# Retention and a gated feed-forward layer in one kernel: k and q of two pairs loaded ahead of v, first gates in halves of 256 tokens, idle products of 128 columns

## The chip, the cores and the metric

The kernel runs on one core of a Trainium2 chip. A core has five engines that run beside each other and meet at semaphores: TensorE (PE in the profile; its weight loads are PEld), VectorE (DVE), ScalarE (ACT), GpSimd (POOL) and SyncE (SP), which here only issues DMAs. SBUF is the working memory, PSUM holds the accumulators of TensorE in banks of 512 float32 numbers per partition. The metric is the device time of one execution in microseconds (us).

## The reference

Retention: 8 batches, 8 heads, 576 positions, 64 numbers per head. Then a feed-forward layer on the 4608 tokens of 512 numbers.

```python
scores = scale * np.matmul(q, k.transpose(0, 1, 3, 2))
Dmat = np.where(rel >= 0, gamma[:, None, None] ** rel[None, :, :], 0.0)
attn_out = np.matmul(scores * Dmat[None, :, :, :], v)
x = attn_out.transpose(0, 2, 1, 3).reshape(B * S, H * D)
gate = 1.0 / (1.0 + np.exp(-(x @ w_gate)))
val = x @ w_val
out = (gate * val) @ w_out
```

The decay `gamma ** (i - j)` is a product of a factor for the query's position and one for the key's, so the kernel multiplies q and k by tables once, and only needs a triangular mask inside a chunk of 128 positions and a running state (k transposed times v) between chunks.

## The kernel before, in words

The work has two parts. The **opening** takes the first 768 tokens as three *pairs* of two chunks each (`PAIRS`: batch 0 positions 0 to 255, batch 0 positions 256 to 511, batch 1 positions 0 to 255), and while they run the weights come in. The **main loop** (L789) takes the other tokens in blocks of 256 to 512, and between pieces of a block's feed-forward work it runs the retention of later chunks (`STEPS`, numbered from 0) by a list (`order`).

The order in each engine's queue is the order of the Python code: nothing is scheduled automatically. Every engine takes its instructions in that order, and a wait holds back all that stands behind it on the engine.

All loads go through SP's queue (L105, L114, L126, L132), each of 256 KB. `load_pair` (L109) is a generator that yields after each load: k, q, k, q, v, v of a pair (two halves of the heads). Before, the queue is: the six of pair 0, the six of pair 1, then the weights for blocks 0 and 1 (`load_w(0, 2)`), for 2 and 3, 4 to 7, 8 to 11, then `wo` mixed with pair 2, then the loads of the steps.

For a pair the opening does these things, with g the half of the heads and a the chunk:
- `cast_pair` (L232): k times its table on GpSimd, q times its table on DVE, v to bf16 on GpSimd.
- `turn` (L599, through `pair_t`, L306): four TensorE products against the identity turn k or q round, ACT copies the result to SBUF (kT, qT).
- `pair_qk` (L323): 16 products of k and q into two banks, then two DVE products with the mask `trip` (L335) give `ptp`.
- `pair_intra` (L361): `ptp` times v into `pvp`; `pair_inter` (L375) adds the state of the chunk before times q.
- `pair_st` (L338): 16 products add this chunk to the state `st`; `tile_sv` (L351) copies the state to SBUF with two copies, and the next `pair_st` may not write until they are done.
- `pair_out` (L383): `pvp` to `xT`, the input of the feed-forward layer, by one engine or in halves by DVE and ACT.

`fill(n)` (L154) issues n products of a zero tile, 128x128 by 128x512, into a fresh bank of the pool `ffn`; nobody reads them. They occupy TensorE where it would otherwise stand.

`h_both` (L602) does the feed-forward's first half for the first 512 tokens: for each of the 12 blocks of 128 of the 1536 hidden numbers, four products of 512 columns with `w_gate` (`hg`) and a sigmoid on ACT, and four with `w_val` (`hv`) and a DVE product of both. Blocks 0 and 1 (L683 to L687) have `pair_st(1, 1)` between their first and second group; blocks 2 and 3, 4 to 7 and 8 to 11 follow (L694, L699, L718). `cast_w` (L216) turns the loaded weights to bf16 just ahead; the second half of `wv` for blocks 0 and 1 is cast by DVE (L681). Beside blocks 8 to 11 pair 2 is turned (L721 to L729), and `op_first` (L742) does the output product with `wo`.

After its casts of `wo`, GpSimd goes on with the steps: `cast_k`, `cast_q` and `cast_v` (L244 to L274) fill `qk_nat` and `vbd`, SP issues a DMA transpose of `qk_nat` into `T` (`cross`, L285), and TensorE's `phase_qk` (L391) multiplies on `T`. PSUM has eight banks: one for `tr`, two for `qk`, one for `pv`, one for `st` and three for `ffn`.

The functions that the diff touches follow.

Of the kernel before, what the change touches and what calls it, by code (L numbers as in the profile page):

```python
# [9 lines left out]
FP32 = mybir.dt.float32  # L10
BF16 = mybir.dt.bfloat16
# [5 lines left out]
def kernel(  # L17
# [91 lines left out]
    def load_pair(A):  # L109

        b, a2 = PAIRS[A]
        for nm, src, g in (("k", k, 0), ("q", q, 0), ("k", k, 1), ("q", q, 1), ("v", v, 0), ("v", v, 1)):
            t = ld_pool.tile([P, M, 2, D], FP32, tag="ld", name=f"{nm}32p_{A}_{g}")
            nc.sync.dma_start(  # L114
                out=t.rearrange("p h r d -> p h (r d)"),
                in_=src[b, g * M:(g + 1) * M, a2 * 2 * P:(a2 + 1) * 2 * P, :].rearrange("h (p r) d -> p h (r d)", r=2))
            parts[nm, "pair", A, g] = t
            yield
# [13 lines left out]
        nc.sync.dma_start(out=t, in_=moe_w_out[f * P:(f + 1) * P, :])  # L132
        parts["o", f] = t

    for A in range(2):
        for _ in load_pair(A):
            pass
    load_w(0, 2)
    load_w(2, 2)
    load_w(4, 4)  # L140
# [7 lines left out]
    LEAD_CAST = 3  # L148


    blank = consts.tile([P, 512], BF16)
    nc.vector.memset(blank, 0.0)

    def fill(n):  # L154

        ps = ffn_psum.tile([P, 512], FP32, tag="ffn", name=f"idle_{fill.at}")
        fill.at += 1
        for i in range(n):
            nc.tensor.matmul(ps, lhsT=blank[:, 0:P], rhs=blank, start=True, stop=True)  # L159

    fill.at = 0
    fill(10)
    def tables(shape, pattern, step, put):

# [67 lines left out]
    def cast_pair(nm, A, g, eng):  # L232

        if (nm, A) not in natural:
            natural[nm, A] = osb_pool.tile([P, 2, H, D], BF16, tag="osb", name=f"{nm}p_{A}")
        o = natural[nm, A][:, :, g * M:(g + 1) * M, :].rearrange("p r h d -> p h r d")
        i = parts.pop((nm, "pair", A, g))
        if nm == "v":
            eng(out=o, in_=i)
        else:  # L240
            tab = (ktab2 if nm == "k" else qtab2)[:, PAIRS[A][1], g * M:(g + 1) * M, :].unsqueeze(3).to_broadcast([P, M, 2, D])
            eng.tensor_tensor(out=o, in0=i, in1=tab, op=ALU.mult)
# [58 lines left out]
    def half(x):  # L301
        return slice(x * 64, x * 64 + 64)
# [20 lines left out]
    def pair_qk(A, g, banks):  # L323
        ps = [psum.tile([P, 2, 2, P], FP32, tag=tag, name=f"qkp_{A}_{g}_{hh}") for hh, (psum, tag) in enumerate(banks)]
        for i in range(2):
            m = 2 * g + i
            for r in range(2):
                for a in range(2):
                    for hh in range(2):
                        nc.tensor.matmul(ps[hh][half(a), i, r, :], lhsT=turned["kp", A][half(hh), m, r, half(a)],  # L330
                                         rhs=turned["qp", A][half(hh), m, a * P:(a + 1) * P], start=True, stop=True)
        if g == 0:
            probs["p", A] = att_pool.tile([P, 2, M, 2, P], BF16, tag="ptp", name=f"ptp_{A}", bufs=1)
        for hh in range(2):
            nc.vector.tensor_tensor(out=probs["p", A][:, hh, 2 * g:2 * g + 2], in0=ps[hh],  # L335
                                    in1=trip.unsqueeze(1).to_broadcast([P, 2, 2, P]), op=ALU.mult)
# [21 lines left out]

    pair_ps = {}

    def pair_intra(A, g, a):  # L361
        s = 2 * A + a
        if g == 0:
            pair_ps[s] = (tr_psum if a else pv_psum).tile([P, M, P], FP32, tag="tr" if a else "pv", name=f"pvp_{s}")
        ps = pair_ps[s]
        for i in range(2):
            m = 2 * g + i
            for r in range(2):
                for hh in range(2):
                    nc.tensor.matmul(ps[half(hh), m, :], lhsT=natural["v", A][half(a), r, 2 * m + hh, :],  # L370
                                     rhs=probs["p", A][half(a), hh, m, r, :],
                                     start=(m == 0 and r == 0), stop=(m == M - 1 and r == 1),
                                     skip_group_check=True)

    def pair_inter(A, a):  # L375
        b, a2 = PAIRS[A]
        c = 2 * a2 + a
        for m in range(M):
            nc.tensor.matmul(pair_ps[2 * A + a][:, m, :], lhsT=state[b, c - 1, 1][:, m, :],
                             rhs=turned["qp", A][:, m, a * P:(a + 1) * P],  # L380
                             start=False, stop=(m == M - 1), skip_group_check=True)

    def pair_out(A, a, eng):  # L383
        t0 = (2 * A + a) * P
        if eng is not None:
            eng(out=xT[:, :, t0:t0 + P], in_=pair_ps[2 * A + a])
            return
        for g, half_eng in enumerate((on_dve, on_act)):
            half_eng(out=xT[:, 2 * g:2 * g + 2, t0:t0 + P], in_=pair_ps[2 * A + a][:, 2 * g:2 * g + 2])

    def phase_qk(s):  # L391
        n = width[STEPS[s][1]]
# [206 lines left out]
    def turn(nm, A, g, pool=ffn_psum, tag="ffn"):  # L599
        pair_t(nm, A, g, pool, tag, on_act)  # L600
# [20 lines left out]
        for _ in range(n):  # L621
            next(units)

    cast_pair("k", 0, 0, nc.gpsimd)
    cast_pair("q", 0, 0, nc.vector)
    cast_pair("k", 0, 1, nc.gpsimd)
    cast_pair("q", 0, 1, nc.vector)
    cast_pair("v", 0, 0, on_pool)
    cast_pair("v", 0, 1, on_pool)
    cast_pair("k", 1, 0, nc.gpsimd)  # L630
    cast_pair("k", 1, 1, nc.gpsimd)
    cast_pair("v", 1, 0, on_pool)
    cast_pair("v", 1, 1, on_pool)
    QK = [(qk_psum, "qk"), (qk_psum, "qk")]
    turn("k", 0, 0)
    turn("q", 0, 0)
    fill(4)
    turn("k", 0, 1)
    pair_qk(0, 0, QK)
    turn("q", 0, 1)  # L640
    fill(3)
    pair_qk(0, 1, QK)
    pair_intra(0, 0, 0)
    pair_intra(0, 0, 1)
    pair_st(0, 0)
    tile_sv(0, 0, (on_act, on_act))
    cast_pair("q", 1, 0, nc.vector)
    cast_pair("q", 1, 1, nc.vector)
    fill(2)
    turn("k", 1, 0)  # L650
    pair_intra(0, 1, 0)
    pair_intra(0, 1, 1)
    fill(2)
    pair_inter(0, 1)
    turn("q", 1, 0)
    pair_out(0, 0, on_act)
    pair_st(0, 1)
    fill(1)
    turn("k", 1, 1)
    pair_out(0, 1, on_dve)  # L660
    turn("q", 1, 1)
    pair_qk(1, 0, QK)
    tile_sv(0, 1, (on_act, on_act))
    fill(3)
    pair_qk(1, 1, QK)
    fill(1)
    pair_intra(1, 0, 0)
    pair_inter(1, 0)
    pair_intra(1, 0, 1)
    pair_st(1, 0)  # L670
    tile_sv(1, 0, (on_act, on_act))
    fill(2)
    pair_intra(1, 1, 0)
    pair_out(1, 0, on_act)
    pair_intra(1, 1, 1)
    pair_inter(1, 1)
    pair_out(1, 1, None)
    for i in range(2):
        cast_w("g", 0, 2, i, on_pool)
    cast_w("v", 0, 2, 0, on_pool)  # L680
    cast_w("v", 0, 2, 1, on_dve)  # L681

    units = h_both((0, 1))  # L683
    step(units, 1)
    pair_st(1, 1)
    tile_sv(1, 1, (on_act, on_act))
    step(units, 3)  # L687
    for i in range(2):
        cast_w("g", 2, 2, i, on_pool)
    cast_w("v", 2, 2, 0, on_pool)  # L690
# [143 lines left out]
```

## Time and profile before

| what | value |
|---|---|
| median of 4 runs | 337.01 us (336.96 to 337.23) |
| the profiled execution: its own time, its span | 337.23 us, 335.5 us |
| PE busy in the span | 326.2 us (97%) |
| DVE, ACT, POOL busy | 164.1, 168.3, 185.9 us |
| granted TensorE clock | 1.00 |
| PE busy from 5.0 to 19.7 us | 12.34 of 14.70 us |
| PE busy from 23.7 to 41.9 us | 18.15 of 18.20 us |
| PE busy from 41.9 to 57.7 us | 15.19 of 15.80 us |

All later times are counted from the start of the span. The page gives the busy share of each engine and the chain of work that ended last; the timeline gives instructions in order of time, with the idle time of the engine before them and what ended it in brackets. A row such as `x4` merges four instructions: its second number is from the start of the first to the end of the last. "SPq" rows are issues of DMAs; the landing of a DMA is told by its time to landing, or by who waited for it.

### The profile page before, as it was taken

What the parts mean: (1) busy time and instruction counts of PE and PEld (TensorE: products, weight loads), DVE (VectorE), ACT (ScalarE), POOL (GpSimd) and SP (SyncE); (2) the same over time, 40 slices, a digit from 0 to 9 for tenths busy, and PEclk for the clock granted to TensorE, in tenths of its full rate; (3) what the DMA queues carried; (4) which work ended last, traced back from release to release, by engine and by line L of the source; (5) the groups of instructions that cost most, each with busy time, mean ns of one, the idle gap of its engine ahead of it and who ended that gap; (6) DMA issues with size and microseconds to landing.
All of it is one profiled execution on the core that took longest, in us unless ns stands there. A gap on an engine that the chain in (4) does not pass through costs nothing.

```text
span 335.5 us, 7361 instructions
## 1 busy us (share of the span) xinstructions
PE 326.2 (97%) x2749; PEld 184.7 (55%) x2784; DVE 164.1 (49%) x328; ACT 168.3 (50%) x345; POOL 185.9 (55%) x327
## 2 busy tenths in 40 slices
PE   8899999999999999999999999999999999999996
PEld 3544445969666566556566555454555455454443
DVE  6644755726376356436346635542674156503320
ACT  6545635637565456355456655445646455233321
POOL 4665769789878978773448976482577500000000
PEclk9999999999999999999999999999999999999999
DMA  8999996999999999999986999499773850020002
GB/s 215 314 374 364 323 259 126 153 214 209 170 221 187 171 209 210 213 225 225 218 151 123 193 247 190 100 229 249 136 137 81 252 205 2 0 95 33 0 31 96
DMA packets 164100, 60.00 MB, mean 179 GB/s; under 512 B 144480, under 2 KB 156000, under 8 KB 164064
## 3 DMA queue, kind: packets, MB, share of 16 engines
q1 hardware_dynamic: 163920, 59.39, 85.1%
q8 instruction: 22, 0.36, 0.5%
q14 instruction: 14, 0.11, 0.1%
q10 hardware_dynamic: 144, 0.13, 0.1%
HBM read 37.75 MB, written 9.44 MB: 141 GB/s over the span
## 4 chain that ended last, share of the span: by engine, by line
PE 93%; DMA 2%; DVE 1%; issue 1%; SPq 1%; ACT 0%; POOL 0%
PE h L495 48%; PE op L561 24%; PE hg L610 3%; PE op L745 3%; PE hv L610 3%; PE pv L420 2%; PE qk L399 2%; PE pv L418 2%; DMA k32p<-in_k_dram 2%; PE st L432 2%; SPq L114 1%; PE op L551 1%; PE pvp L370 1%; PE st L345 0%; PE idle L159 0%
## 5 line engine op out<-in xcount | busy, mean ns | idle before, releaser
L495 PE MATMUL h<-xT,wg_sb 128*128 128x384 bf16 (+2 forms) x476 | 102.4, 336 | 0.4 <-DVE gv L523 0.2
L495 PE MATMUL h<-xT,wv_sb 128*128 128x384 bf16 (+2 forms) x473 | 102.2, 336 | 0.4
L252 POOL TENSOR_TENSOR qk_nat<-k,ktab 64x256 bf16<-64x256 f32 x120 | 73.4, 612 | 42.9 <-PE st L432 27.2
L523 DVE TENSOR_TENSOR gv<-g,h 128x384 bf16<-128x384 bf16 (+1 forms) x96 | 59.6, 621 | 71.8 <-PE h L495 56.0
L561 PE MATMUL op<-wo_sb,gv 128*128 128x512 bf16 x356 | 84.5, 379 | 0.8
L519 ACT ACTIVATE g<-h 128x384 bf16<-128x384 f32 (+1 forms) x96 | 52.3, 545 | 64.7 <-PE h L495 58.1
L438 DVE CAST sbd<-st 64x256 bf16<-64x256 f32 x104 | 43.7, 420 | 45.1 <-PE st L432 42.9
L495 PEld LDWEIGHTS <-wg_sb 128*128 128x128 bf16 x480 | 43.7, 98 | 31.4 <-issue 0.4
L495 PEld LDWEIGHTS <-wv_sb 128*128 128x128 bf16 x480 | 44.1, 98 | 29.0 <-issue 0.4
L273 POOL CAST vbd<-v 64x256 bf16<-64x256 f32 x120 | 47.6, 397 | 14.8 <-PE pv L420 10.3
L561 PEld LDWEIGHTS <-gv 128*128 128x128 bf16 x372 | 34.3, 98 | 36.3
L538 ACT COPY ob<-op 128x512 f32<-128x512 f32 x33 | 19.4, 587 | 47.4 <-PE op L561 39.2
L283 ACT CAST vs<-v 64x256 bf16<-64x256 f32 x104 | 42.1, 405 | 1.6
L262 POOL TENSOR_TENSOR qk_nat<-q,qtab 128x512 bf16<-128x512 f32 (+1 forms) x34 | 35.4, 1041 | 2.6
L422 ACT CAST xT<-pv 128x512 bf16<-128x512 f32 (+1 forms) x34 | 18.2, 535 | 18.1 <-PE pv L420 18.0
L401 DVE TENSOR_TENSOR pt<-qk,tri 128x512 bf16<-128x512 f32 (+1 forms) x34 | 21.2, 625 | 6.1 <-PE qk L399 5.8
L420 PE MATMUL pv<-pt,vbd 128*128 128x64 bf16 x240 | 18.0, 193 | 0.0
L432 PEld LDWEIGHTS <-qk_nat 128*128 128x128 bf16 x208 | 13.2, 98 | 8.7
L420 PEld LDWEIGHTS <-vbd 128*128 128x128 bf16 x240 | 15.2, 98 | 3.6
L418 PE MATMUL pv<-T,sbd 128*128 128x64 bf16 x216 | 17.2, 193 | 0.0
L511 DVE TENSOR_TENSOR gv<-g,h 128x256 bf16<-128x256 bf16 x24 | 10.0, 420 | 13.7 <-ACT g L509 13.4
L418 PEld LDWEIGHTS <-sbd 128*128 128x128 bf16 x216 | 15.1, 98 | 2.5
(76 smaller groups left out, 233.5 us busy)
## 6 DMA issues: line engine op xcount, KB each, us to landing
out_dram<-ob SPq DMA_DIRECT2D x34, 256.0 KB, 2.8
v<-in_v_dram SPq DMA_DIRECT2D x26, 256.0 KB, 4.0
k<-in_k_dram SPq DMA_DIRECT2D x26, 256.0 KB, 4.5
q<-in_q_dram SPq DMA_DIRECT2D x26, 256.0 KB, 5.0
wg<-in_moe_w_gate_dram SPq DMA_DIRECT2D x12, 256.0 KB, 5.7
wv<-in_moe_w_val_dram SPq DMA_DIRECT2D x12, 256.0 KB, 5.4
wo<-in_moe_w_out_dram SPq DMA_DIRECT2D x12, 256.0 KB, 5.4
k32p<-in_k_dram SPq DMA_DIRECT2D x6, 256.0 KB, 5.8
```

What stands on the lines that cost most here:

```text
L252: nc.gpsimd.tensor_tensor(out=kn[half(hh), j, :, half(hh)], in0=k32[half(j), hh::2, :], in1=ktab[half(j), c, hh::2].unsqueeze(2).to_broadc ...
L262: nc.gpsimd.tensor_tensor(out=qs[0:n], in0=q32[0:n], in1=qtab[0:n, c, :].unsqueeze(2).to_broadcast([n, H, D]), op=ALU.mult)
L273: nc.gpsimd.tensor_copy(out=vb[half(hh), j, :, half(hh)], in_=v32[half(j), hh::2, :])
L283: nc.scalar.copy(out=natural["vs", s][half(hh), j], in_=loaded[s][0][half(j), hh::2, :])
L401: nc.vector.tensor_tensor(out=pt[:, :, 0:n].rearrange("p m (j t) -> p m j t", t=64), in0=qkp[:, :, 0:n].rearrange("p m (j t) -> p m j t", ...
L418: nc.tensor.matmul(pvp[:, m, half(j)], lhsT=before[:, m, :], rhs=qT[:, m, half(j)], start=True, stop=False)
L420: nc.tensor.matmul(pvp[:, m, half(j)], lhsT=vb[:, j, m, :], rhs=pt[:, m, half(j)], start=before is None, stop=True)
L438: nc.vector.tensor_copy(out=sb[half(hh), :, half(hh)], in_=st_tiles[b][half(hh)])
L495: nc.tensor.matmul(out, lhsT=w_sb[:, kc, fc * P:(fc + 1) * P], rhs=xT[:, kc, t0 + a:t0 + e], start=(kc == 0), stop=(kc == NKC - 1))
L519: nc.scalar.activation(out=g[:, 0:n], in_=h1[:, 0:n], func=AF.Sigmoid)
L523: nc.vector.tensor_tensor(out=gvs[some[0]][:, a:e], in0=g[:, 0:n], in1=h2[:, 0:n], op=ALU.mult)
L561: nc.tensor.matmul(opp, lhsT=gvs[fc][:, nb * P:(nb + 1) * P], rhs=wo_sb[:, fc, :], start=(fc == 0), stop=(fc == NFC - 1))
```

## The change

It does five things.

1. `load_pair` of pairs 0 and 1 is drawn in turn: k, q, k, q of pair 0, the same of pair 1, then v, v of pair 0 and v, v of pair 1. GpSimd's casts are in that order too: all four k, then all four v, then the weights of blocks 0 and 1, now all four on GpSimd.
2. The opening is written in another order: the turns and `pair_qk` of pair 1 ahead of the products that need v; `pair_qk` alternates between the banks `qk` and `ffn`; the turns use the banks `tr` and `pv`; `pvp` of the last chunk lies in two banks; `ptp` has two buffers.
3. Blocks 0 and 1 of the feed-forward layer are done in halves of 256 tokens (`h_half`, `gate`), the first of them among `pair_inter(1, 1)` and `pair_st(1, 1)`. Sixteen products of 512 columns become 32 of 256.
4. `fill(n)` issues 4 n products of 128 columns, all into one tile. The sum of all n goes from 28 to 21.
5. `pair_out` takes one engine or several, each with its share of the head pairs.

PE's program has 144 rows more (5714 instead of 5570, weight loads counted). The rest of the kernel, from `cast_w("g", 2, 2, ...)` on, is the same text.

```diff
-    for A in range(2):
-        for _ in load_pair(A):
-            pass
+    both = [load_pair(A) for A in range(2)]
+    for n_pair in (4, 2):
+        for one in both:
+            for _ in range(n_pair):
+                next(one)
...
-    blank = consts.tile([P, 512], BF16)
+    blank = consts.tile([P, P], BF16)
...
+    idle = ffn_psum.tile([P, 512], FP32, tag="ffn", name="idle")
+
     def fill(n):
-        ps = ffn_psum.tile([P, 512], FP32, tag="ffn", name=f"idle_{fill.at}")
-        fill.at += 1
-        for i in range(n):
-            nc.tensor.matmul(ps, lhsT=blank[:, 0:P], rhs=blank, start=True, stop=True)
+        for i in range(4 * n):
+            nc.tensor.matmul(idle[:, 0:P], lhsT=blank, rhs=blank, start=True, stop=True)
...
+    def pair_tile(A, a, banks):
+        s = 2 * A + a
+        ps = [psum.tile([P, M // len(banks), P], FP32, tag=tag, name=f"pvp_{s}_{i}") for i, (psum, tag) in enumerate(banks)]
+        pair_ps[s] = [(ps[m * len(banks) // M], m % (M // len(banks)), M // len(banks)) for m in range(M)]
...
+    for A in range(2):
+        for g in range(2):
+            cast_pair("k", A, g, nc.gpsimd)
+    for A in range(2):
+        for g in range(2):
+            cast_pair("v", A, g, on_pool)
+    for i in range(2):
+        cast_w("g", 0, 2, i, on_pool)
+    for i in range(2):
+        cast_w("v", 0, 2, i, on_pool)
+    QK = [(qk_psum, "qk"), (qk_psum, "qk")]
+    FF = [(ffn_psum, "ffn"), (ffn_psum, "ffn")]
+    TR, PV = (tr_psum, "tr"), (pv_psum, "pv")
     cast_pair("q", 0, 0, nc.vector)
+    turn("k", 0, 0, *TR)
+    turn("q", 0, 0, *PV)
+    fill(3)
     cast_pair("q", 0, 1, nc.vector)
     pair_qk(0, 0, QK)
+    turn("k", 0, 1, *TR)
+    fill(2)
+    turn("q", 0, 1, *PV)
     fill(3)
+    cast_pair("q", 1, 0, nc.vector)
+    pair_qk(0, 1, FF)
+    turn("k", 1, 0, *TR)
+    turn("q", 1, 0, *PV)
+    fill(2)
+    cast_pair("q", 1, 1, nc.vector)
+    turn("k", 1, 1, *TR)
+    pair_qk(1, 0, QK)
+    fill(1)
+    turn("q", 1, 1)
     pair_intra(0, 0, 0)
     pair_intra(0, 0, 1)
     pair_st(0, 0)
     tile_sv(0, 0, (on_act, on_act))
     pair_intra(0, 1, 0)
+    pair_qk(1, 1, FF)
     pair_intra(0, 1, 1)
+    pair_st(0, 1)
     pair_inter(0, 1)
     pair_out(0, 0, on_act)
     pair_out(0, 1, on_dve)
     tile_sv(0, 1, (on_act, on_act))
     pair_intra(1, 0, 0)
+    pair_tile(1, 1, QK)
     pair_intra(1, 0, 1)
+    pair_intra(1, 1, 0)
     pair_st(1, 0)
     tile_sv(1, 0, (on_act, on_act))
+    pair_inter(1, 0)
+    pair_out(1, 0, on_dve)
     pair_intra(1, 1, 1)
...
+    g0 = h_bank(ffn_psum, "ffn", "hg_0", 1)[:, 0]
+    h_half("g", 0, 0, g0)
+    gate(0, 0, g0)
     pair_inter(1, 1)
+    pair_out(1, 1, on_dve, on_act)
+    g1 = h_bank(ffn_psum, "ffn", "hg_1", 1)[:, 0]
+    h_half("g", 1, 0, g1)
+    gate(1, 0, g1)
     pair_st(1, 1)
     tile_sv(1, 1, (on_act, on_act))
+    v0 = h_bank(ffn_psum, "ffn", "hv_0", 2)
+    h_half("v", 0, 0, v0[:, 0])
+    h_half("g", 0, 1, (g2 := h_bank(qk_psum, "qk", "hg_2", 2))[:, 0])
+    h_half("g", 1, 1, g2[:, 1])
+    h_half("v", 1, 0, v0[:, 1])
+    gate(0, 1, g2[:, 0])
+    gate(1, 1, g2[:, 1])
+    for fc in range(2):
+        h_half("v", fc, 1, h_bank(ffn_psum, "ffn", f"hv_{1 + fc}", 1)[:, 0])
```

`h_half(what, fc, x, ps)` is four products of 256 columns for half x of the tokens, and for `"v"` the DVE product into `gv`; `gate` is the sigmoid on ACT.

## The prediction

> **What bounds the kernel now.** I read the page first. Its first part and its chain say that this is a TensorE kernel.
>
> ```profile
> PE 326.2 (97%) x2749; PEld 184.7 (55%) x2784; DVE 164.1 (49%) x328; ACT 168.3 (50%) x345; POOL 185.9 (55%) x327
> PE 93%; DMA 2%; DVE 1%; issue 1%; SPq 1%; ACT 0%; POOL 0%
> ```
>
> PE is busy for 97% of the span, so nearly all of it is work that this change leaves alone. Time can only be won where PE stands or runs idle products: the opening. I therefore took the chain of work that ended last, in order of time, for the first 24 us.
>
> ```profile
> 4.05 6.07 DMA k32p<-in_k_dram
> 10.19 1.05 POOL kp L242
> 11.29 0.40 PE kTp L311 x4
> ...
> 19.13 0.44 DVE xT L389
> 19.70 1.02 PE hg L610 x4
> ...
> 23.79 1.73 PE hg L610 x8
> ```
>
> The seventh load (k of pair 1) lands at 4.05 + 6.07 = 10.12, and GpSimd starts on it at 10.19, so 0.07 after a landing its user runs. From there to the first gate product at 19.70 PE strings together pair 1. The gates of blocks 2 and 3 (`hg`, second group) start at 23.63 in the timeline, and from there PE has no wait worth the name until the end: the waits of PE after 57 us add up to 0.2 us. So what counts is, first, how much earlier that second group starts, and second, whether anything later holds PE at a fixed time. For the second question I read the timeline of GpSimd and of SP's issues from 46 to 58 us.
>
> ```profile
> 46.31 0.61 POOL L224 CAST wo_sb<-wo 128x512 bf16<-128x512 f32 x1 [0.79 <-DMA wo<-in_moe_w_out_dram]
> ...
> 47.67 1.84 POOL L781 MEMSET vbd<- 128x1024 bf16 x2
> 49.59 2.66 POOL L252 TENSOR_TENSOR qk_nat<-k,ktab 64x256 bf16<-64x256 f32 x4
> 52.32 1.04 POOL L262 TENSOR_TENSOR qk_nat<-q,qtab 128x512 bf16<-128x512 f32 x1
> ```
> ```profile
> 53.39 1.54 SPq L289 DMA_TRANSPOSE T<-qk_nat  x1
> ```
> ```profile
> T<-qk_nat SPq DMA_TRANSPOSE x1, 3.8
> ```
> ```profile
> 57.72 0.40 PE L399 MATMUL qk<-T 128*128 128x64 bf16 x8
> ```
>
> This is a chain without PE in it. GpSimd waits for the last `wo` load, casts it, clears two tiles, casts k and q of the first later step, and SP issues the transpose when the q cast ends (52.32 + 1.04 = 53.36). The transpose takes 3.8 us to land (DMA view of that window): 57.2. PE's first `qk` on it starts at 57.72. **PE reaches that product with only 57.72 - 57.2 - 0.07 = 0.45 us to spare.**
>
> **The change part by part.**
>
> *Order of loads.* All twelve are 256 KB in the same pattern, so I take the landings by place in the queue. Starts of the casts that waited for DMA in the trace: 3.75, 4.57, 6.00, 7.42, 8.37, 9.25, 10.19, about 11.05, 12.01, 12.84, 13.74, 14.59, then the first weights at 15.46. k and q of pair 1 thus come at 8.37 to 11.05 instead of 10.19 to 12.84, v of pair 0 at 12.01 and 12.84 instead of 8.37 and 9.25. Weights keep their places.
>
> *The opening, recomputed.* The turns and masks of both pairs now run while v is on its way: PE meets kp(1,1) at 10.19 + 1.04, qp(1,1) on DVE at about 12.1, and the last turn copy (0.74) ends near 13.4. From v a chain follows: v cast 12.84 + 0.61 = 13.45; 16 state products 0.44, 13.95; two copies of the state 0.75, 14.7; next state 0.44, 15.2; on ACT the xT copy 0.59 stands ahead, so the copies run 15.3 to 16.05; third state to 16.55; its copies to 17.3; inter 0.40; xT halves 0.42 and 0.37, 18.2. Beside it the masks of (1,1) end at 15.6 (two of 0.64 each after PE's products at 14.1), which frees the two DVE copies of xT by 17.5.
>
> *Gates of 256 tokens.* The first needs xT of pair 0 (16.3) and the wg casts, which end at 15.46 + 1.37 = 16.83 as before: it runs 16.9 to 17.35 between the state products, where PE would stand. The second wv cast moves from DVE (19.48 in the trace) to GpSimd behind the first (16.96 + 0.61) and its landing: about 18.3. So the first value product starts at 18.35 instead of 21.90. Thirty-two products of 256 columns replace sixteen of 512: four of 256 take 0.44 from start to start (L495 rows near 56 us), so 8 x 0.44 = 3.5 against 3.45, nothing. Six groups are left at 18.35: 18.35 + 6 x 0.44 = 21.0. **The second group of gates starts at 21.0 instead of 23.63: a lead of 2.6 us.** ACT gets four sigmoids of 0.39 for two of 0.60 and DVE four products of 0.42 for two of 0.69: 0.36 and 0.3 us more, beside PE, whose next use of those tiles is 20 us off; without that cover they would cost as much.
>
> *Idle products.* Twenty-eight of 512 columns become 84 of 128, so a quarter of the number times 3. The first ten units take the same 4.45 us (kTp of 128 columns start 0.107 apart in the slow stretch, a fourth of 0.43); a smaller `blank` (0.27 us now, at least the 0.06 of a small memset) brings them up to 0.2 forward, which the load of k(0,1) at 6.00 swallows. I take 0; both ends are 0 to -0.2.
>
> *Banks, `bufs=2`, one idle tile.* They take away waits on accumulators within the opening and issue nothing. Cost 0, already in the times above.
>
> *What takes the lead back.* At 37.44 PE turns k of pair 2; its cast starts at 34.70 and ends at 35.74, behind GpSimd's memset and the landing, with no PE in it. PE comes there at 37.44 - 2.6 = 34.85 and waits to 35.8: the lead is now 1.64. At `qk` of step 0 it would be at 57.72 - 1.64 = 56.08, but the transpose lands at 57.2, so PE goes on at 57.27. **Of 2.6 us, 0.95 go at the turn, 1.19 at the transpose, and 0.45 are left.** The third transpose (issued 63.09, 4.1 us) lands at 67.2; PE wants it at 67.74 - 0.45 = 67.29, just in time. The others have over a microsecond of room. After that PE hands the 0.45 through to the end.
>
> Sum: the profiled execution took 337.23 (span 335.5, 1.7 around it); 337.23 - 0.45 = 336.78. It stands 0.22 above the median of 337.01, so against the median I say **336.6**. That is 0.13%, under the 0.2% (0.67 us) that a measurement of this kernel can about tell from no change.
>
> *The unknown: when the transpose lands.* Its age in the window 50 to 75 us is 3.3 to 4.7 us, so 0.5 less or 0.9 more than the 3.8 I use. And the program's own instruction blocks (queue 8: 22 packets, 0.36 MB) go through the same DMA engines. The one at 20.5 to 21.9 was followed by a wg cast that waited 0.91 and started at 23.59, 2.18 after the pair before it at 21.41, where later pairs (24.95, 26.31, 27.66, 29.01) stand 1.35 apart; so a block can cost a load some 0.8; the one near 12.5 moved nothing. The change adds 144 rows to PE's 5570, all before the gates, so each block is asked for earlier: by row number I place them near 10, 15, 24.5 and 44 us in place of 12.5, 20.8, 39.7 and 49.6. Three blocks before the last `wo` load become four, but one leaves the neighbourhood of that load. Bounds: the load 0.85 later or 0.85 earlier; I keep 0, between them. [...]
>
> *The clock.* The idle products start 0.43 us apart up to 6.2 us and 0.217 after it ((1.03 - 0.38) / 3 in the row of four at 6.25), so PE does run at half speed at first. After the last fill (about 12.2 us) the new order holds under 3 us of PE work in the 4.7 us up to the gates. [...] In the trace PE stood up to 0.5 us at a time between 6 and 20 us without its products getting slower; the longest stand that I foresee is 0.7, so I count no loss. From the two spacings, 16 gate products of 512 at 0.43 instead of 0.217 would cost 3.4 us, the far end.
>
> **Rivals.**
>
> - *The gate moves forward* (20%). The block near 40 us no longer delays the last loads, the transpose lands 0.4 to 0.85 earlier, PE gains 0.85 to 1.3: 335.7 to 336.2. For: the loads before 46 are one unbroken stream. Against: the new block near 44 us.
> - *The lead passes* (8%): PE keeps 1.64 or more: 335.4 or below. It needs the transpose 1.2 earlier, and nothing in GpSimd's chain gets shorter.
> - *A block falls on the last `wo` load or on the transpose itself* (15%), at 44 to 46 us or 53 to 57. Price 0.85 to 1.75 (one block, or one and the longest transpose age); from 0.45 on it is slower than before. One block: +0.4, 337.4; with the long transpose +1.3, 338.3.
> - *The opening doesn't get shorter* (7%), by the clock or by a wait that I missed: if the lead at the gates is under 0.45, the gain is what is left, 0; with the clock halved through the gates 3.4 - 2.6 = 0.8 slower, 337.8.
>
> **How the numbers follow.** The forecast (gain 0 to 0.67) has 50%. Faster by over 0.2%: the forward gate, the passed lead and a few in a hundred from the forecast's edge, 0.31. Slower by over 0.2%: half of the third rival and part of the last, 0.13. Within: 0.56. The range takes the forward gate in up to a 1.1 us gain and the one-block loss, 335.9 to 337.5.
>
> **What would show it.** The second group of gates starts at 21 to 22; `kTp` of pair 2 waits for GpSimd near 35; PE stands about 1 us before the first `qk` of L405, released by the DMA of T; after it every PE row is 0.4 to 0.5 earlier than before. I am wrong if PE doesn't stand there, if the last `wo` cast leaves 46.3 by more than half a microsecond, or if the gates start after 23.

## The result and the profile after

The changed kernel takes **338.34 us** (median of 52 runs, 336.52 to 339.58) against 337.20 of the kernel before beside it (72 runs, 336.62 to 338.61): the ratio is 1.0031, with a 95% interval of 1.0024 to 1.0037. It is slower, by about 1.1 us, where 336.6 had been forecast.

The median hides two groups. Each execution records its mean granted TensorE clock. Of the 53 on record, the profiled one among them, 19 have 1.00, and their median is 337.44 us; in 33 it is 0.985 to 0.990, and their median is 338.69; one lies between. None of the 128 executions of the kernel before that ran beside the experiments has a clock under 0.998. So there are two losses: about 0.2 us with the clock full (337.44 against 337.20), and 1.2 us more (338.69 - 337.44) wherever the clock falls, which is in six executions of ten.

The execution profiled for the page was one at full clock: 337.44 us, span 335.7. Its busy line and its chain by engine are:

```profile
PE 325.3 (97%) x2824; PEld 190.1 (57%) x2856; DVE 165.2 (49%) x330; ACT 168.5 (50%) x346; POOL 186.3 (55%) x328
PE 80%; DMA 11%; POOL 3%; SPq 2%; issue 1%; DVE 1%; ACT 0%
```

TensorE works 0.9 us less than before (325.3 against 326.2), and the span is 0.2 us longer. The chain has moved from TensorE to the transfers: DMA held 2% of it, now 11%. The timeline of TensorE shows where (start, duration, engine, line, operation, tiles, shape, count; in brackets the idle time before it and what ended it).

```profile
13.66 0.37 PE L346 MATMUL st<-vp,kp 64*64 64x64 bf16 x12 [0.55 <-POOL vp L240]
21.39 1.89 PE L616 MATMUL hg<-xT,wg_sb 128*128 128x512 bf16 x7
36.61 0.40 PE L312 MATMUL kTp<-ident,kp 128*128 128x128 bf16 x4 [1.20 <-POOL kp L243]
40.40 0.38 PE L312 MATMUL qTp<-ident,qp 128*128 128x128 bf16 x4 [0.36 <-ACT qT L322]
57.92 0.41 PE L405 MATMUL qk<-T 128*128 128x64 bf16 x8 [0.34 <-DMA T<-qk_nat]
```

The second group of gates starts at 21.39 instead of 23.63: the opening did get 2.24 us shorter. Then TensorE stands 1.20 us for the cast of k of pair 2, 0.36 for a copy at the turn of its q, and 0.34 for the first transpose, and meets that transpose's product at 57.92, where before it was at 57.72. By the starts of the rows, before and after, the lead goes 1.41 us at the first place, 0.53 at the second and 0.50 at the third. **A lead of 2.24 us has become a lag of 0.20**, and the profiled execution ends 0.21 later (337.44 against 337.23). The last row, in the chain of work that ended last (start, duration, engine, what):

```profile
53.54 4.33 DMA T<-qk_nat
57.92 0.41 PE qk L405 x8
```

SP issues the transpose 0.15 later than before (53.54, 53.39), and it is in flight for 4.33 us instead of 3.8.

That is the loss at full clock. The other one, the clock, cannot be seen in this profile at all; the first experiment was to catch it.

### The profile page after: what moved, and what is told of

It reads as the page before. It is cut to its first block, busy times and chain, and to the rows that moved or that the text cites. A ratio compares the mean times of both kernels' runs of the same rounds, so it can differ in the third digit from the quotient of the medians.

```text
span 335.7 us, 7513 instructions
## 1 busy us (share of the span) xinstructions
PE 325.3 (97%) x2824; PEld 190.1 (57%) x2856; DVE 165.2 (49%) x330; ACT 168.5 (50%) x346; POOL 186.3 (55%) x328
## 3 DMA queue, kind: packets, MB, share of 16 engines
HBM read 37.75 MB, written 9.44 MB: 141 GB/s over the span
## 4 chain that ended last, share of the span: by engine, by line
PE 80%; DMA 11%; POOL 3%; SPq 2%; issue 1%; DVE 1%; ACT 0%
PE h L501 48%; PE op L567 24%; DMA wv<-in_moe_w_val_dram 5%; DMA wo<-in_moe_w_out_dram 3%; SPq L114 2%; PE pv L426 2%; PE qk L405 2%; PE pv L424 2%; PE st L438 2%; DMA v32p<-in_v_dram 2%; DMA T<-qk_nat 1%; PE op L557 1%; POOL qk_nat L253 1%; POOL vbd L816 1%; POOL vbd L746 1%
```

## The experiments

In the table, "full" counts executions with a mean clock of 0.997 or more, "one" those at 0.994 or 0.995, "more" those at 0.990 or less. The records of the clock in the traces explain these steps: the clock is halved for stretches of 3.41 (a7_512), 6.83 (a10_stand), 10.24 (a1_same) or 13.65 us (b1_thin), whole multiples of 3.41, and 0.5 x 3.41 of some 338 us is 0.005. The last column is the ratio to the kernel before on the same chip, with its 95% interval.

| run | full | one | more | median at full clock | median | ratio |
|---|---|---|---|---|---|---|
| changed kernel | 19 | 1 | 33 | 337.44 | 338.34 | 1.0031 (1.0024 to 1.0037) |
| a1_same | 4 | 0 | 8 | 336.98 | 338.25 | 1.0028 (1.0007 to 1.0049) |
| a2_fill | 11 | 0 | 0 | 337.86 | 337.86 | 1.0007 (0.9997 to 1.0017) |
| a3_open | 6 | 0 | 6 | 336.65 | 337.67 | 1.0009 (0.9991 to 1.0027) |
| b1_thin | 0 | 0 | 5 | none | 340.92 | 1.0112 (1.0095 to 1.0128) |
| a5_hole | 10 | 0 | 2 | 337.00 | 337.10 | 0.9998 (0.9981 to 1.0016) |
| a6_oldload | 3 | 4 | 5 | 337.87 | 338.29 | 1.0040 (1.0020 to 1.0061) |
| a7_512 | 4 | 8 | 0 | 336.90 | 337.74 | 1.0006 (0.9992 to 1.0021) |
| b2_open | 12 | 0 | 0 | 337.25 | 337.26 | 0.9997 (0.9988 to 1.0007) |
| a8_open_wide | 11 | 0 | 1 | 336.77 | 336.81 | 0.9981 (0.9964 to 0.9998) |
| a9_wide | 8 | 0 | 4 | 337.36 | 338.05 | 1.0014 (0.9995 to 1.0032) |
| a10_stand | 0 | 0 | 8 | none | 339.27 | 1.0047 (1.0030 to 1.0064) |
| a11_open_wide3 | 11 | 1 | 0 | 337.06 | 337.07 | 0.9981 (0.9965 to 0.9997) |
| a13_gate512 | 5 | 0 | 7 | 337.65 | 339.39 | 1.0052 (1.0024 to 1.0080) |
| a14_first512 | 8 | 1 | 3 | 337.01 | 337.23 | 1.0006 (0.9989 to 1.0023) |

Three mechanisms compete in the expectations; each expectation says which it means by its names or numbers. **The clock**: TensorE has too little work in some stretch of the opening, and its clock is halved for a while (3.41 to 13.65 us in the traces); from a5_hole on, theory 1 says that the one stand ahead of the first state products decides this, against the thin stretch as a whole. **The middle**: the turns of pair 2 and the first transpose take the lead back. **The code blocks** (theory 3): the instructions that the DMA engines fetch (queue 8 on the page: 22 packets, 0.36 MB, so 16 KB each, and 0.5% of the time of the same 16 engines) make a load or a transpose late. They are taken for TensorE's own code, since they come by the number of its instructions: with 60 fewer ahead, the first block moved from 10.51 us (a3_open) to 12.60 (a14_first512).

### a1_same: the changed kernel again, and its profile with the halved clock

No edit.

> The changed kernel once more, for the clock of each of its executions. Theory (clock): the share of executions in which the granted TensorE clock falls in the opening is what makes it slower; the runs should split in two groups, clock about 1.00 near 337.4 us and clock about 0.99 near 338.6 us, while the kernel before stays at 1.00. Rival (gate and code blocks): the time is set by when the first transpose lands; then runs of equal clock should still spread over 2 us, and the clock should not sort them.

Eight of twelve fell, and the clock sorts the times, as the clock theory expected: the four at full clock took 336.60 to 337.30 us, the others 338.07 to 340.88. The median of those four, 336.98, is under the 337.29 of the kernel before beside them, so the loss of 0.2 us at full clock is not the same in every round. This time the profiled execution, 340.88 us, is one that fell. Below are two answers on its trace. First the busy times in windows of 3.41 us laid on the stretches of the clock records (window, its length, busy time of each engine with the count, then the granted clock, the DMA share and GB/s):

```profile
8.72:12.14 3.42, 3.05 (x62) 2.71 (x60) 3.36 (x7) 2.26 (x4) 2.09 (x2) 1.00 1.09 291
12.14:15.55 3.41, 1.76 (x48) 1.33 (x49) 1.92 (x4) 1.61 (x3) 1.03 (x2) 1.00 0.94 266
15.55:18.96 3.41, 3.17 (x86) 2.85 (x87) 1.75 (x3) 2.05 (x5) 2.65 (x5) 0.50 0.98 313
18.96:22.38 3.42, 3.42 (x46) 2.68 (x43) 1.14 (x3) 1.21 (x4) 2.82 (x5) 0.50 1.03 351
22.38:25.79 3.41, 3.41 (x31) 2.26 (x30) 0.54 (x2) 1.40 (x4) 2.45 (x5) 0.50 1.03 375
25.79:29.20 3.41, 3.41 (x24) 2.22 (x23) 1.62 (x4) 1.25 (x3) 1.89 (x4) 1.00 1.02 359
```

Then the rows around the hole, from the timelines of TensorE and of GpSimd, and the second group of gates:

```profile
15.13 0.61 POOL L240 CAST vp<-v32p 128x512 bf16<-128x512 f32 x1 [1.71 <-DMA v32p<-in_v_dram]
...
15.79 0.53 PE L346 MATMUL st<-vp,kp 64*64 64x64 bf16 x12 [1.85 <-POOL vp L240]
...
27.28 1.89 PE L616 MATMUL hg<-xT,wg_sb 128*128 128x512 bf16 x8
```

The second v of the first pair lands 2.1 us later than in the page's execution (its cast starts at 15.13, there at 13.00), TensorE stands 1.85 us instead of 0.55 ahead of the first state products, and works only 1.76 us of that window's 3.41. With the next window the clock is 0.50, and stays there for 10.24 us, though TensorE is now busy for 3.17, 3.42 and 3.41 us of the three windows. The second gates start at 27.28 instead of 21.39. Of these 5.9 us, 2.24 are the lead. The rest passes the middle whole, for the first transpose lands 3.2 us before its product needs it: against before, the gates are 27.28 - 23.63 = 3.65 late, and the execution is 340.88 - 337.23 = 3.65 longer.

### a2_fill: idle products put back among the state products

```diff
     pair_intra(0, 0, 1)
+    fill(2, idle2)
     pair_st(0, 0)
...
     pair_intra(0, 1, 1)
+    fill(1, idle2)
     pair_st(0, 1)
...
+    fill(1, idle2)
     pair_intra(1, 0, 0)
...
     pair_intra(1, 1, 0)
+    fill(1, idle2)
     pair_st(1, 0)
...
     pair_intra(1, 1, 1)
+    fill(1, idle2)
```

> The changed kernel with six more units of idle products (24 of 128 columns, 1.3 us of TensorE) among the state products of the opening. Clock theory: all executions at 1.00, about 337.3 us, 1 us faster than the changed kernel. Rival (gate and code blocks): same as the changed kernel, 338.3, or 0.2 slower.

The clock is full in all eleven. But at 337.86 the kernel is not faster than before. TensorE's timeline in its profile says why: the first transpose is met at 57.33, 0.39 before the kernel before, and then a stand comes at the third one, which had not been there.

```profile
57.33 0.41 PE L405 MATMUL qk<-T 128*128 128x64 bf16 x8 [0.24 <-DMA T<-qk_nat]
68.28 0.29 PE L405 MATMUL qk<-T 128*128 128x64 bf16 x4 [0.76 <-DMA T<-qk_nat]
```

The third transpose was issued at 63.18 and landed at 68.23, 5.05 us in flight; in the changed kernel it was 63.24 to 66.56. By the DMA records a block of TensorE's code was fetched at 64.56 here, in that flight, and at 68.45 there. The 24 extra products are 48 more instructions ahead of it.

### a3_open: the way through the middle opened

The clears of the value tiles go to VectorE and ahead, and the turns of pair 2 come one gate group later.

```diff
-    for t in vbd[0:2]:
-        nc.gpsimd.memset(t, 0.0)
+    for t in vbd:
+        nc.vector.memset(t, 0.0)
...
-    step(units, 4)
+    step(units, 5)
     cast_wo(2, on_pool)
     turn("k", 2, 0, tr_psum, "tr")
...
     turn("q", 2, 1, pv_psum, "pv")
-    step(units, 1)
...
-    for t in vbd[2:4]:
-        nc.gpsimd.memset(t, 0.0)
```

> The changed kernel with the gates opened: the four clears of vbd on DVE instead of GpSimd, and the turns of pair 2 one group of products later. Clock theory alone: the executions with the lower clock stay, about 337.9 (only the 0.3 to 1 us that the turn and the transpose took back comes out). Rival (gate): the lead passes, about 336.5 to 337.0, 1.3 us or more faster than the changed kernel.

At full clock it takes 336.65, 0.6 under before: the lead passes. The product of the first transpose starts at 56.73, one microsecond before the kernel before's 57.72. But six of twelve executions fall, to 338.60, so the median is no better. The two losses are separate, and each has to be mended.

### b1_thin: the kernel before, without its idle products after the first ten units

All `fill(n)` after `fill(10)` are removed, nothing else.

> The kernel before without its idle products after the first ten (18 units of 512 columns left out). Clock theory: a share of the executions drops to a clock of 0.99 and the median rises to 338 or more. Rival: the idle products only cover waits, 337.1 as before or 0.2 less.

All five fall, and the profiled one has the clock at 0.50 from 11.98 for 13.65 us. So the old order falls too once it is thin: TensorE stood 1.55 us ahead of 7.54 and 0.82 ahead of 9.44, and the two windows before the fall held 1.85 and 2.02 us of work.

### a5_hole: a3_open, and two units of idle products at one place

```diff
     pair_intra(0, 0, 1)
+    fill(2, idle2)
     pair_st(0, 0)
```

> The changed kernel with the edits of a3_open (all four clears of the value tiles on VectorE, the turns of pair 2 one gate group later), and two units of idle products (8 x 128 columns, 0.43 us) ahead of the first state products, where TensorE stood 0.55 us (profile of after), 0.93 (a3_open) and 1.85 (a1_same, the one with the halved clock) for the cast of the last v of pair 1. Theory 1 (that one stand is what halves the clock): the clock is full in all or nearly all executions, where a3_open had it in 6 of 12; the median is then a3_open's at full clock, 336.65, up to 0.3 more: 336.6 to 337.0, ratio 0.998 to 0.9995. Theory 2 (the thin stretch as a whole, 5 to 17 us, does it): 0.43 us more work in twelve changes little, 4 to 8 of 12 executions fall, median 337.3 to 338.3.

(The cast called that of the last v of pair 1 is that of the second v of the first pair, L240.) Ten of twelve at full clock, where a3_open had six: eight products of 128 columns at this one place do nearly what a2_fill's 24 did. Its median at full clock is 0.35 above that of a3_open (ten executions against six, and their ranges overlap), and in its profile it is again the third transpose, with a code block fetched at 65.71:

```profile
67.85 0.29 PE L405 MATMUL qk<-T 128*128 128x64 bf16 x4 [0.79 <-DMA T<-qk_nat]
```

### a6_oldload: the loads in the old order

```diff
-    both = [load_pair(A) for A in range(2)]
-    for n_pair in (4, 2):
-        for one in both:
-            for _ in range(n_pair):
-                next(one)
+    for A in range(2):
+        for _ in load_pair(A):
+            pass
```

> The changed kernel with one part undone: loads in the old order (k, q, k, q, v, v of pair 1, then of pair 2). v of the first pair then lands four loads earlier (about 3 us), k of the second two loads later (about 1.5 us). Theory 1 (the new order of loads makes the stand ahead of the first state products, and that halves the clock): that stand goes, but one of 1 to 2 us comes ahead of the turn of the second pair's k; if any such stand does it, the clock falls at least as often and the median is 338 to 339.5; if only a stand of the last v does it, the clock is full and the time is 337.3 to 338.2 by the later opening. Theory 2 (the gate at the middle, no clock): the lead is gone before it starts, 337.3 to 337.9 with the clock full.

The stand moves, as theory 1 expected, to the turn of the second pair's k:

```profile
11.42 0.40 PE L310 MATMUL kTp<-ident,kp 128*128 128x128 bf16 x4 [1.45 <-POOL kp L241]
58.38 0.41 PE L403 MATMUL qk<-T 128*128 128x64 bf16 x8 [0.44 <-DMA T<-qk_nat]
```

Nine of twelve executions have a halved window or more, and the three at full clock have a higher median than the changed kernel's (337.87). The order of loads is not the fault by itself: with few idle products a late operand made a hole at either place (1.85 us in a1_same, 1.45 here), and the order of loads only chose the place.

### a7_512: the idle products 512 columns wide again

```diff
-    blank = consts.tile([P, P], BF16)
+    blank = consts.tile([P, 512], BF16)
...
-        for i in range(4 * n):
-            nc.tensor.matmul(idle[:, 0:P], lhsT=blank, rhs=blank, start=True, stop=True)
+        for i in range(n):
+            nc.tensor.matmul(idle, lhsT=blank[:, 0:P], rhs=blank, start=True, stop=True)
```

> The changed kernel with its idle products 512 columns wide as before (one in place of four, the same columns in all). Theory 1 (the stand, not the form of the idle products): the clock falls in about 6 of 10 executions as in after, median 338.0 to 338.6. Theory 3 (the 63 fewer TensorE instructions move the 16 KB blocks of its code to later work; the block at 10 to 12 us is what makes the last v land late on one DMA engine, by 1.4 us more in a1_same): the block falls behind that load, the stand stays under 0.5 us, the clock is full in most executions, and the median is 336.9 to 337.5.

Neither theory foresaw this. No execution falls by more than one window, but eight of twelve fall by one. In the profile the code block came at 15.63 instead of 9.93, the v was in time (stand 0.41), and then TensorE stood 2.17 us ahead of a state product for nothing that the trace shows, right behind the start of that fetch:

```profile
18.19 0.22 PE L346 MATMUL st<-vp,kp 64*64 64x64 bf16 x2 [2.17 <-issue]
```
```profile
15.43:18.84 3.41, 1.24 (x38) 0.95 (x34) 0.52 (x2) 0.51 (x3) 1.76 (x4) 1.00 1.09 347
18.84:22.26 3.42, 3.42 (x38) 2.34 (x35) 1.05 (x2) 1.73 (x5) 2.20 (x5) 0.50 1.06 379
```

That TensorE waited there for its own code is the reading that fits; the trace does not name it, and its DMA records have the block's transfer ended at 16.75, 1.4 us before TensorE went on. The window's 1.24 us of work and the halved clock behind it are theory 1 once more, with another cause for the stand.

### b2_open: the edits of a3_open on the kernel before

> The kernel before with the gate edits of a3_open alone (all four clears on VectorE, the turns of pair 2 one gate group later). By the theory that the shorter opening is worth something only once the middle lets it through, and the edits only once there is a lead, nothing waits here that they could free: ratio 0.999 to 1.001, clock full. By the rival (the edits are a gain of their own, and the opening gives nothing) it is as much faster as a3_open at full clock, 0.6 us, ratio 0.998.

337.26, ratio 0.9997: nothing. The edits in the middle are worth 0.6 us behind a shorter opening and nothing without one.

### a8_open_wide: the same fill in two instructions

```diff
     pair_intra(0, 0, 1)
+    for _ in range(2):
+        nc.tensor.matmul(idle2, lhsT=blank, rhs=natural["k", 0][:, 0].rearrange("p h d -> p (h d)"), start=True, stop=True)
     pair_st(0, 0)
```

> a5_hole with its eight idle products of 128 columns written as two of 512 (weights of zeros, the right side is the first k, already there): the same 0.43 us of work at the same place, but 4 TensorE instructions more than a3_open in place of 16. In a2_fill and a5_hole a 16 KB block of TensorE's code was fetched at 64.56 and 65.71 us, in the flight of the third transpose, and TensorE stood 0.76 and 0.79 for it; in a3_open it came at 67.24 and there was no such stand. Theory 1 with 3 (clock by the stand, the rest of a5_hole's loss by the block's place): clock full in 9 or more of 12, no stand at the third transpose, median 336.5 to 336.9, ratio 0.997 to 0.999. Rival (the eight products cost what they take, or the stand at the third transpose is only the lead's end): 336.9 to 337.2 as a5_hole.

Eleven of twelve at full clock, median 336.81, ratio 0.9981: faster than both kernels. The code block came at 68.82, and the third transpose landed 1.76 us before its product. What limits now is the first transpose, 5.06 us in flight, with a block at 53.23:

```profile
14.22 0.38 PE L346 MATMUL st<-vp,kp 64*64 64x64 bf16 x12 [0.57 <-POOL vp L240]
21.95 1.89 PE L616 MATMUL hg<-xT,wg_sb 128*128 128x512 bf16 x7
57.25 0.41 PE L405 MATMUL qk<-T 128*128 128x64 bf16 x8 [0.89 <-DMA T<-qk_nat]
```

### a9_wide: the two wide products without the edits in the middle

The diff of a8_open_wide alone on the changed kernel.

> The changed kernel with the two wide idle products of a8_open_wide alone, without the edits at the gate. By theory 1 the clock is full in 9 or more of 12, and what is left is the changed kernel at full clock, 337.0 to 337.5: ratio 0.999 to 1.001, no gain over before, since the middle takes the opening's lead back. By theory 2 for the clock (the thin stretch as a whole) it falls in half the executions, 337.8 to 338.5.

At full clock 337.36 beside 337.42 of before: without the edits in the middle no gain, as expected. The clock is full in eight of twelve, one short of the nine that theory 1 asked and two above the six of theory 2, so this count does not part the two. In the profiled execution GpSimd waited 1.71 us for the second v, so that 1.17 us of stand was left behind the fill; that execution still kept its clock, with 1.92 us busy in the window.

### a10_stand: the stand made longer

```diff
     for A in range(2):
         for g in range(2):
+            if (A, g) == (0, 1):
+                for t in vbd[0:2]:
+                    nc.gpsimd.memset(t, 0.0)
             cast_pair("v", A, g, on_pool)
```

> The changed kernel with GpSimd clearing two value tiles (0.95 us each, once more, their later clears stay) ahead of its cast of the second v of the first pair: the stand of the first state products grows from 0.55 us by some 1.5 to about 2.0, in every execution. Theory 1: the clock falls in 10 or more of 12; median 338.5 to 340. Theory 2 (a stand of this kind is harmless, the clock goes by something else that differs between executions): it falls in about 6 of 10 as in after, and the median is at 338.2 to 338.8, or the lost 1.5 us shows with the clock full in many.

All eight executions fall. The window with the stand holds 1.31 us of work, and the next two are at half clock:

```profile
12.31 1.84 POOL L637 MEMSET vbd<- 128x1024 bf16 x2
14.11 0.61 POOL L240 CAST vp<-v32p 128x512 bf16<-128x512 f32 x1
...
14.77 0.38 PE L346 MATMUL st<-vp,kp 64*64 64x64 bf16 x12 [1.87 <-POOL vp L240]
...
25.19 1.89 PE L616 MATMUL hg<-xT,wg_sb 128*128 128x512 bf16 x7
```
```profile
12.50:15.91 3.41, 1.31 (x64) 1.09 (x65) 1.00 (x3) 1.44 (x3) 2.85 (x5) 1.00 1.12 330
15.91:19.32 3.41, 3.34 (x70) 2.82 (x71) 1.87 (x4) 2.03 (x6) 2.89 (x5) 0.50 1.08 345
19.32:22.74 3.42, 3.42 (x38) 2.35 (x35) 0.95 (x2) 1.38 (x5) 2.24 (x5) 0.50 1.06 375
22.74:26.15 3.41, 3.36 (x28) 2.67 (x28) 1.95 (x5) 1.19 (x4) 2.85 (x5) 1.00 1.05 377
```

The gates start 25.19 - 23.63 = 1.56 later than before, and this execution took 338.77, 1.54 more than the profiled one of before. In this execution the second v itself landed only at 14.05, as the clears ended, so it would have had much the same stand without them. What the edit does is to keep the stand from being short in any execution: the clears end at 14.15 even where v lands at 12.95, as it did in the changed kernel's profile. So it is the count that makes theory 1 more than a reading: six falls in ten became eight in eight, which by the old share would come about in 2 of 100 such runs. The clears hold back GpSimd's later casts too, so the edit is not of this stand alone.

### a11_open_wide3: three wide products

The diff of a8_open_wide with `range(3)`.

> a8_open_wide with three wide idle products, 0.64 us, at the same place. If two leave some executions with too long a stand, three take these as well, and the clock is full in 11 or 12 of 12; if the products cost time of their own it is up to 0.2 us slower than a8_open_wide at full clock: 336.6 to 337.1.

No execution fell by more than one window; 337.06 at full clock, ratio 0.9981, the same as with two.

### a13_gate512: the first gates in one piece of 512 tokens

The half gates of blocks 0 and 1 are replaced by `units = h_both((0, 1))` behind both pairs, in the order of before.

> The changed kernel with the first gates and values of blocks 0 and 1 in one piece of 512 tokens again, behind both pairs. The second gates then start later by what the halves brought: TensorE has about 1.8 us of gate work less to do ahead of the last state products. The stand of the first state products is as in after, so the clock falls in about 6 of 10 (theory 1). At full clock: if the halves make most of the lead, it is gone before the middle, and the time is 337.2 to 338.0 at full clock, as the profile of after has no room to lose; if the new order of loads and products alone makes it, 336.9 to 337.5.

Seven of twelve fall, as in the changed kernel. At full clock it is 337.65. In its profile the stand was 1.55 (clock full all the same: it lies from 13.05 to 14.60, across the border of two windows at 13.78, which hold 2.45 and 2.29 us of work) and the second gates started at 23.17; with the 0.55 of the changed kernel's profile that would be 22.2. By that estimate the half gates bring about 0.8 of the 2.24 us, the new order of loads and products the rest. Where a stand falls among the windows thus seems to count beside its length: in the profiles the first window at full clock begins anywhere from 3.95 to 7.20 us. No run was made to test this.

### a14_first512: the code block moved, the work unchanged

a3_open with the first ten units of idle products, ahead of everything, as ten of 512 columns in place of 40 of 128.

```diff
-    fill(10)
+    for i in range(10):
+        nc.tensor.matmul(idle, lhsT=blank[:, 0:P], rhs=blank, start=True, stop=True)
```

> a3_open with the first ten units of idle products as ten of 512 columns in place of 40 of 128: the same columns, 30 products (60 TensorE instructions with their weight loads) fewer ahead of everything, the later idle products unchanged. By instruction number the first 16 KB block of TensorE's code, fetched at 10.51 us in a3_open, moves to about 13 to 14.5. Theory 3 (the block, fetched while the second v of the first pair is in flight, makes one DMA engine late with it: its lag rose by 0.4 to 1.4 us there in every profile with the block at 10.1 to 12.1, and not in a7_512 with the block at 15.63): v lands in time, TensorE's stand ahead of the first state products is 0.5 us or less, and the clock is full in 9 or more of 12 (a3_open 6 of 12), with 336.3 to 336.9; a later block can again make a stand of its own, as in a7_512. Rival (the lag comes from the loads themselves): stand 0.9 and more, clock full in about half, 337.3 to 338.3.

The block came at 12.60, and in the rows of GpSimd the second v is on time, and the fourth is now the late one.

```profile
13.15 0.62 POOL L241 CAST vp<-v32p 128x512 bf16<-128x512 f32 x1 [0.29 <-DMA v32p<-in_v_dram]
14.06 0.62 POOL L241 CAST vp<-v32p 128x512 bf16<-128x512 f32 x1 [0.30 <-DMA v32p<-in_v_dram]
15.68 0.62 POOL L241 CAST vp<-v32p 128x512 bf16<-128x512 f32 x1 [1.00 <-DMA v32p<-in_v_dram]
```

A load lands in 16 parts, and its cast waits for the last: in the changed kernel's profile those of the second v land from 11.35 to 12.95, and the cast starts at 13.00. The distance from the middle part to the last was 0.86 for the second v here and 1.64 for the fourth. In a1_same it jumped from 1.76 to 3.18 at the second v (block at 12.11), in a9_wide from 1.45 to 2.87 (11.50), in a10_stand from 0.49 to 1.96 (11.01), in a8_open_wide from 0.42 to 1.24 (10.46), in a3_open from 1.15 to 1.70 (10.51); it did not jump in the changed kernel's profile (block at 9.93), nor in a7_512 (15.63), a5_hole (9.99) and the kernel before (12.53). So not every block makes a load later, and a1_same was 1.76 behind, where the changed kernel's profile was 0.94, before its block came. The stand was 0.43 us, and the clock full in eight of twelve and halved for one window in a ninth, nine asked for: theory 3 fits this profile, and the count, eight or nine against six of twelve, is too small a difference to prove it by itself. At full clock it takes 337.01, more than the 336.3 to 336.9 expected.

## Why the prediction was wrong, point by point

- **The opening.** Right in direction, a little too hopeful: 21.39 for the second gates instead of the 21.0 worked out, a lead of 2.24 instead of 2.6.
- **The turn of k of pair 2.** Right in kind: the stand ahead of `kTp` is there, 1.20 us. The cast that it waits for ended at 36.55 instead of 35.74, so 37.44 - 36.61 = 0.83 of the lead is kept and 1.41 lost, where 0.95 had been taken. Of the 0.81, 0.52 came from ahead of the clears, where the last `wv` was waited for, and the rest from two casts that took 0.79 and 1.21 us instead of 0.61 and 1.04. The next stand, 0.36 at the turn of q, was missed.
- **The first transpose.** The mechanism was right and two sizes were off. The chain on GpSimd was taken as unmoved and was 0.15 later; the transpose was given 3.8 us and took 4.33. 0.15 + 0.53 make the 0.68 between the 0.45 gain forecast and the 0.21 loss of this execution, less 0.02 of rounding. The rival "a block falls on the transpose" was therefore the better forecast for full clock, with some luck in the size (its price was 0.85, measured were 0.53 and 0.15): it said 337.4, and the profiled execution took 337.44, with a block fetched at 54.26, inside the flight.
- **The failed step: "The clock ... I count no loss."** The sum had a stand of 0.7 us at most and priced the loss at nothing. In the profiled execution the stand was 0.55, so that the row looked right, but it is a different length in each execution: 0.55, 0.93, 1.55, 1.85 in four profiles without a fill there. Windows of 3.41 us with 1.31 us of work (a10_stand) and 1.76 (a1_same) were followed by half the clock, and the halved stretch was 6.8 and 10.2 us long. The reading of before that the step leaned on was short too: the longest stand there up to 20 us was 0.61, ahead of 19.70, and not 0.5. The price of a fall is not taken up at the transpose: in a1_same the first transpose landed 3.2 us ahead of its product, so all that the opening loses behind the 23.63 of before reaches the end. The rival that has the clock (the opening does not get shorter, 7%) was right in kind and too small: it said 337.8, and the executions that fell have a median of 338.69 and are six in ten.
- **The shift of the code blocks** had bounds of 0.85 and was put at the last `wo` load. Blocks did move, and about to the places worked out (9.93, 18.05, 23.27 and 45.03 for 10, 15, 24.5 and 44); the next came at 54.26. What was not foreseen is what they may cost in the opening, beside the second v, where the price is the clock. Over the profiles of the study the first transpose took 3.77 to 3.84 us where no block was fetched in its flight (seven of sixteen profiles, before among them), 4.27 to 5.06 where one was (changed kernel, a3, a6, a8, a9, a11), and 3.78 to 3.80 where the block came in its first or last quarter of a microsecond (a5, b1, a10).

Shown by edits: that the clock goes with the stand ahead of the first state products (a10_stand lengthens it, 8 of 8 fall; with a fill at that place, a2, a5, a8, a9 and a11 together, 7 of 59 executions fall by more than a window, without it, the changed kernel, a1, a3 and a13, 54 of 89, and with a14, whose edit is elsewhere, 57 of 101); that the middle takes the lead back (a3_open against b2_open). Not separated: whether it is the place of the fill or its 0.43 us of work that counts, since no run puts the same fill elsewhere in the opening. Argued from profiles: that the fill's number of instructions moves the loss at the third transpose (a5 against a8, whose times at full clock overlap); that a code block makes the second v later, which a14_first512 supports in its profile and not clearly in its count, and that TensorE stood for its own code in a7_512.

## What to carry to other kernels

Idle products that keep a clock up (without those behind the first ten units it fell in five of five executions, b1_thin) are a part of the order and not padding: when operands are moved, look for the place where the last of them lands, and put the fill there; by the profiles, though not clearly by the times, few wide products serve better than many narrow ones. Two products of 512 columns ahead of the first state products, with the clears and the turns in the middle moved out of the way, made 336.81 of a kernel at 338.34, and 0.9981 (0.9964 to 0.9998) of the one before. One profile at full clock says little about a kernel whose clock falls in some executions only (here six in ten): look at the granted clock of every execution before the rows are read.

## What the runs showed of the hardware

- In the profiles the granted clock went only between 1.00 and 0.50, in steps of 3.41 us: in a1_same it was 1.00 from 5.31 and 0.50 from 15.55 to 25.79, in a7_512 1.00 from 5.19 and 0.50 from 18.84 to 22.26. The windows just ahead of a fall held 1.24 (a7_512), 1.31 (a10_stand), 1.76 (a1_same) and, in b1_thin behind one of 1.85, 2.02 us of TensorE work. Windows with 1.81 in a6_oldload, 1.90 in a1_same (5.31 to 8.72) and in a11_open_wide3, and 1.92 in a9_wide did not bring one, so busy time in one window is not the whole rule, and what is stays open.
- The clock came back after one halved window in a7_512, two in a10_stand, three in a1_same and four in b1_thin. A full window did not always bring it back at once: in a1_same it stayed halved behind windows of 3.17 and 3.42 us of work and came back after the third, of 3.41.
- More TensorE instructions went with earlier code blocks: with 16 more, weight loads included, a block came 1.5 us earlier (67.24 in a3_open, 65.71 in a5_hole), in a transpose's flight, and TensorE then stood 0.79 us. With 4 more (a8_open_wide) it came at 68.82, so the number is not all that places it.
